# Attention and gated MLP in one kernel: the second product of a head pair issued in two runs, its V load and its x^T store placed later

## The chip, the cores and the metric

The kernel runs on one NeuronCore of a Trainium2 chip. The metric is the device time of one execution in microseconds (us). Engines are named as in the profile: PE (matrix engine, with PEld for its weight loads), DVE (vector), ACT (scalar), POOL (GpSimd) and SP (which here only issues DMAs).

## The reference

Causal attention in blocks of 64, then a gated MLP without biases, all in float32:

```
scores = q @ k^T / sqrt(64), masked where block(query) < block(key)      # 8 batches, 8 heads, 576 x 64
attn   = exp(scores - max) / (sum + 1e-9)
x      = (attn @ v), heads side by side                                    # 4608 x 512
out    = (sigmoid(x @ w_gate) * (x @ w_val)) @ w_out                        # 512 -> 1536 -> 512
```

## The kernel before

Matrix operands are split into a high and a low part and a product is summed from three matmuls (high by high, high by low, low by high), so that 128x512 matmuls run in a fast form and keep precision. The names end in H and L for the two parts.

**Stages.** The heads are taken in 32 pairs (two heads of one batch). The loop over pairs near the end of the kernel runs one period for each pair. While attention runs, matmuls of the MLP's first four column chunks are dealt in between (L153 for gate and value, L160 for the output product), at a rate worked out from what is left over the places ("ticks") of a period. After the last pair the rest of that MLP part follows, and then the remaining eight chunks in ten passes (L1110, L1195).

**Order of a period.** The tables at the top (lines 28 to 36) write out the order by hand: a name and the number of ticks of MLP work dealt after it. Pairs 0 to 6 go by `FIRST` and `ALONE`, pair 7 by `TURN`, pair 8 by `JOIN`, pairs 9 to 31 by `REST`. The steps of a `REST` period are these.

- `AV`: the product of the previous pair's probabilities with V (`z_av`, L583). `s`: this pair's scores (`s_blocks`), on PE, with a mask, a row maximum (L434) and exponentials on ACT (L442) behind them. `t`: the scores of the last 64 queries, the tail (L307 with operands QBH and QBL), which need the bank of the first scores again and so wait for its exponentials.
- `tr3`, `tr2`, `trl`, `trt`: DVE transposes of the probabilities of query blocks 3, 2, 1 with 0, and the tail into the tile Z (L568, L576, L579). Z and one of the two V buffers lie in one tile, ZV; the other V buffer is VR1. Even pairs use VR1, odd pairs the one in ZV.
- `k` and `q`: the next pair's K and Q are transposed on DVE and split on ACT and DVE (L341, L378 to L383), and the loads of K and Q for the pair three further on are issued.
- `r`: the reciprocals of the sums (L494 to L499), written to DRAM (r_d, L502) and read back spread over the partitions (rb, L507 and L508).
- `FX`: `finish` of the previous pair: POOL multiplies x^T by rb (L629), ACT splits off the high part (L631), the store of x^T to DRAM is issued on ACT's queue (L636), and POOL makes the low part (L638).

**Queues.** A scheduler orders the instructions of each engine. `behind(a, b)` forbids it to place a ahead of b on the same engine, and `line(engine, a)` chains the instructions of an engine in program order. On PE the scores, the dealt MLP matmuls and the AV product are chained in that way. The V load (L246, two heads into 32 partitions, then L248 copies them to the other 96) has no such tie, nor has the store of x^T.

**AV.** Each pair takes 18 key blocks of 32 keys, four row groups and two heads, so 144 matmuls, each recorded as two matmul and two weight-load instructions, into four PSUM banks:

```
order = [*range(4), 16, 17, *range(4, 16)]
for n, kb in enumerate(order):
    ...
            matmul(pv[a // 2][rows(h), a % 2, lo:144], lhsT=VR[at_rows, h, kb],
```

**Later weights.** In the first five passes, `do_later` (L1263) converts 24 pieces of the weights of the second five, and stores them to DRAM (wgv_d, wo_d). Its count is by place of the pass and by unit in it. After the fifth pass the output weights are loaded from wo_d into the one tile wo (L1328), which the sixth pass needs.

Of the kernel before, what the change touches and what calls it, by code (L numbers as in the profile page):

```python
# [20 lines left out]
N2 = 512  # L21
# [10 lines left out]
JOIN = (("s", 3), ("t", 1), ("AV", 2), ("tr3", 1), ("tr2", 1), ("k", 0), ("trl", 1), ("trt", 1), ("r", 0), ("q", 3))  # L32
REST = (("AV", 0), ("s", 3), ("t", 3), ("tr3", 1), ("tr2", 1), ("k", 0), ("FX", 0), ("trl", 1), ("trt", 1), ("r", 0), ("q", 2))
# [9 lines left out]
def attn_glu_kernel(ctx: ExitStack, tc: tile.TileContext, q, k, v, w_gate, w_val, w_out, out):  # L43
# [142 lines left out]
    with ExitStack() as s2:  # L186
# [53 lines left out]
        def load(p, what, queue=nc.sync):  # L240
            b, hp = pairs[p]
            h0 = 2 * hp
            if what == "v" and p > N_FIRST:
                VR = VRs[(p + 1) % 2]
                for h in range(2):
                    nc.sync.dma_start(out=VR[0:32, h], in_=v[b, h0 + h].rearrange("(t p) d -> p t d", p=32))  # L246
                for a in range(1, 4):
                    dma = nc.sync.dma_start(out=VR[32 * a:32 * a + 32], in_=VR[0:32])  # L248
                loads["SP"] = dma.ins
                return  # L250
# [151 lines left out]
        def attend(p):  # L402
# [88 lines left out]
            def recip():  # L491
# [12 lines left out]
                if rest:  # L504
                    tails = r_f[4 * P:5 * P].rearrange("(a h r) -> a h r", a=4, h=2)
                    for h in range(2):
                        nc.sync.dma_start(out=rb[rows(h), 0:4 * P], in_=r_f[5 * P * h:5 * P * h + 4 * P].partition_broadcast(D))  # L507
                        nc.sync.dma_start(out=rb[rows(h), 4 * P:S].rearrange("p (a r) -> p a r", a=4),  # L508
                                          in_=tails[:, h].partition_broadcast(D))
                    return  # L510
                for h, o, n, f in ((0, 0, S, 0), (1, 4 * P, D, S), (1, 0, 4 * P, S + D)):
                    dma = nc.sync.dma_start(out=rb[rows(h), o:o + n], in_=r_f[f:f + n].partition_broadcast(D))
                rb_last[:] = [dma.ins] if p < N_FIRST else []
# [69 lines left out]
            def z_av():  # L583
                pv = [two_banks(), two_banks()]
                VR = VRs[(p + 1) % 2]
                order = [*range(4), 16, 17, *range(4, 16)]
                for n, kb in enumerate(order):
                    g = kb // 4
                    lo, z = (32 * g, ZB * (kb % 4) + (ZG + 32) * g) if g < 4 else (P, 2 * P + 16 * (kb % 4))
                    for a in range(4):  # L590
                        at_rows = slice(32 * a, 32 * a + 32)
                        for h in range(2):
                            matmul(pv[a // 2][rows(h), a % 2, lo:144], lhsT=VR[at_rows, h, kb],
                                   rhs=Z[at_rows, ZH * h + z:ZH * h + z + 144 - lo],
                                   start=(n == 0), stop=(n == len(order) - 1), tile_position=(32 * a, 64 * h))
                            if n == a == h == 0:
                                for ins in recent:
                                    behind(pe_last[0], ins)
                hold[:] = pe_last
                for t, (engine, copy) in enumerate((("ACT", nc.scalar.copy), ("DVE", nc.vector.tensor_copy))):  # L600
# [23 lines left out]
            def finish():  # L624
# [9 lines left out]
                if p == len(pairs) - 1:  # L634
                    mark("ACT", cut)
                (nc.sync if NP <= p <= N_FIRST else nc.scalar).dma_start(  # L636
                    out=xT_d[b, hp * P:(hp + 1) * P, :], in_=xT)
                nc.gpsimd.tensor_sub(out=XL[:, hp, :w], in0=xT[:, :w], in1=XH[:, hp, :w].bitcast(F32))  # L638
# [11 lines left out]
            def step(what):  # L650
# [18 lines left out]
                elif rest and what == "trt":  # L669
                    z_tail()  # L670
                elif what == "tr3":
# [10 lines left out]
                elif what == "av":  # L682
                    if rest:
                        z_av()
                        return
# [577 lines left out]
        def do_later(k, i):  # L1263

            place = turns_of[0].index(k)
            count = 2 * (0 if place == 0 or blocks[k][1] < N2 else i < 4 if place == 1 else i in (0, 1, 3) if place == NK - 1
                         else 1)
# [90 lines left out]
```

## Time and profile before

| | us |
|---|---|
| median of 3 runs | 1306.68 |
| lowest and highest run | 1300.39, 1309.89 |
| profiled execution, time | 1306.74 |
| profiled execution, span of the core's instructions | 1305.0 |
| PE busy in it | 1156.9 (89%) |
| periods of pairs 9 to 31 with the end of pair 8's, about | 145.5 to 655.3 |

The time of the profiled execution stands 1.7 us above its span, and at the median of the runs. An engine's busy time is a sum over stages with different limits, so what a change is worth is read from the stage in which it lies. "Idle before" in a row is the time in which an engine stood still ahead of those instructions, with what ended it; "issue" means that nothing the profile shows was waited for.

### The profile page before, as it was taken

The page shows a single profiled execution, that of the slowest core. Times are in us where ns is not written, and L with a number is a line of the kernel's source. Part 1 is how long each engine was busy: PE and PEld are TensorE (multiplying, and loading weights), DVE is VectorE, ACT ScalarE, POOL GpSimd, SP SyncE. Part 2 cuts the span into 40 slices and gives each one's busy share as a digit, 9 for nine tenths or more (in the row PEclk, how much of TensorE's full clock was granted, in tenths as well). Part 3 has the DMA queues.
Part 4 walks back from the last instruction along what each step waited for, and adds up shares of the span by engine and source line. Part 5 has one row for each costly group of instructions (what it writes and reads, how often), then busy time and mean ns, then how long its engine had stood idle before and what let it go on. Part 6 is the DMA issues. An engine that isn't in the chain of part 4 may idle for free.

```text
span 1305.0 us, 30506 instructions
## 1 busy us (share of the span) xinstructions
PE 1156.9 (89%) x12073; PEld 934.8 (72%) x12073; DVE 928.4 (71%) x1844; ACT 547.0 (42%) x1274; POOL 334.9 (26%) x380
## 2 busy tenths in 40 slices
PE   8799788877688878787798999999999969999998
PEld 5466576666566656665676888888888758888888
DVE  5778666665575757565788695887988876767665
ACT  5677444343343434252424444354454422333222
POOL 3355332222231322222330120111120133342502
PEclk9899999998899989889999999999999989999999
DMA  7666555655555546463523314264277747262532
GB/s 167 170 147 154 122 127 128 135 121 123 112 112 140 115 109 144 95 141 92 152 84 109 117 49 130 49 192 131 69 208 264 250 161 234 67 208 89 178 98 80
DMA packets 314687, 175.31 MB, mean 134 GB/s; under 512 B 239152, under 2 KB 279088, under 8 KB 311600
## 3 DMA queue, kind: packets, MB, share of 16 engines
q1 hardware_dynamic: 303744, 154.84, 47.0%
q10 hardware_dynamic: 10416, 17.47, 3.8%
q8 instruction: 95, 1.56, 0.5%
q0 software_dynamic: 384, 1.05, 0.2%
q14 instruction: 48, 0.39, 0.1%
HBM read 104.73 MB, written 47.33 MB: 117 GB/s over the span
## 4 chain that ended last, share of the span: by engine, by line
PE 55%; DVE 16%; DMA 11%; issue 8%; SPq 4%; ACT 4%; POOL 2%; ACTq 0%; DVEq 0%; POOLq 0%
PE b L1110 21%; PE bank L307 10%; PE m L153 6%; PE b L1195 6%; PE m L1195 6%; DVE ZV L568 3%; DMA rb<-r_d 3%; PE m L160 2%; DMA r_d<-rT 2%; ACT P L442 2%; DMA part_d<-ost 1%; SPq L278 1%; POOL xT L629 1%; SPq L502 1%; DVE KQ L341 1%
## 5 line engine op out<-in xcount | busy, mean ns | idle before, releaser
L1110 PE MATMUL b<-XH,w 128*128 128x512 f32 (+1 forms) x1120 | 321.9, 369 | 1.9 <-DVE p L1156 0.5
L1110 PEld LDWEIGHTS b<-XH,w 128*128 128x128 f32 x1120 | 203.5, 188 | 40.3 <-DVE p L1156 1.4
L1110 PE MATMUL b<-XL,w 128*128 128x512 f32 (+1 forms) x560 | 205.8, 368 | 0.0
L442 ACT ACTIVATE P<-bank,nm 128x512 f32<-128x512 f32 (+3 forms) x256 | 131.8, 538 | 122.0 <-POOL xT L629 74.7
L1110 PEld LDWEIGHTS b<-XL,w 128*128 128x128 f32 x560 | 105.6, 189 | 17.4
L942 ACT CAST XH<-XB 128x1024 fp32r<-128x1024 f32 (+1 forms) x72 | 67.2, 945 | 94.6 <-DVE XB L940 49.4
L434 DVE TENSOR_REDUCE nm<-bank 128x2 f32<-128x1024 f32 (+3 forms) x128 | 102.5, 822 | 3.1
L1195 PE MATMUL m<-wo,hH 128*128 128x512 f32 x288 | 95.0, 396 | 10.2 <-DMA wo<-wo_d 10.2
L307 PE MATMUL bank<-ZV 32*64 32x144 f32 (+5 forms) x3680 | 76.5, 264 | 28.2 <-issue 28.2
L160 PE MATMUL m<-wo,hH 128*128 128x512 f32 x256 | 90.2, 419 | 12.3 <-DVE h L172 9.7
L307 PEld LDWEIGHTS bank<-ZV 32*64 32x64 f32 (+1 forms) x3680 | 62.7, 136 | 45.7 <-issue 34.2
L1195 PE MATMUL b<-wo,hH 128*128 128x512 f32 x288 | 93.0, 389 | 0.0
L153 PE MATMUL m<-XH,wv 128*128 128x512 f32 x240 | 85.5, 415 | 4.9 <-ACT t L170 4.1
L945 DVE TENSOR_TENSOR XL<-XB,XH 128x1024 fp32r<-128x1024 f32 (+1 forms) x72 | 80.1, 1115 | 13.7 <-ACT XH L942 12.0
L927 POOL TENSOR_TENSOR XB<-XB 128x256 f32<-128x256 f32 x30 | 23.7, 790 | 251.1 <-DMA XB<-xT_d 126.1
L601 DVE COPY xT<-bank 128x256 f32<-128x256 f32 x24 | 10.2, 425 | 107.7 <-PE bank L307 107.7
L153 PE MATMUL m<-XH,wg 128*128 128x512 f32 x240 | 83.3, 404 | 1.8 <-ACT ost L778 1.8
L568 DVE STREAM_TRANSPOSE ZV<-P 128x512 f32<-128x512 f32 (+1 forms) x192 | 80.1, 476 | 0.0
L629 POOL TENSOR_TENSOR xT<-xT,rb 128x576 f32<-128x576 f32 x24 | 34.0, 1417 | 169.5 <-DMA rb<-r_d 80.8
L1195 PEld LDWEIGHTS m<-wo,hH 128*128 128x128 f32 x288 | 55.2, 192 | 22.2 <-DMA wo<-wo_d 10.6
L160 PEld LDWEIGHTS m<-wo,hH 128*128 128x128 f32 x256 | 51.6, 203 | 27.1 <-DVE h L172 11.8
L485 DVE TENSOR_REDUCE nm<-bank 128x1 f32<-128x576 f32 x32 | 24.2, 756 | 65.3 <-PE bank L307 65.3
(214 smaller groups left out, 2535.4 us busy)
## 6 DMA issues: line engine op xcount, KB each, us to landing
XB<-xT_d SPq DMA_DIRECT2D x48, 256.0 KB
prr<-part_d SPq DMA_DIRECT2D x46, 256.0 KB
VR<-VR SPq DMA_DIRECT2D x36, 288.0 KB
ZV<-ZV SPq DMA_DIRECT2D x36, 288.0 KB
part_d<-ost SPq DMA_DIRECT2D x36, 256.0 KB
part_d<-ost ACTq DMA_DIRECT2D x32, 256.0 KB
xT_d<-xT ACTq DMA_DIRECT2D x28, 288.0 KB
rqk<-in_k_dram SPq DMA_DIRECT2D x108, 72.0 KB
```

What stands on the lines that cost most here:

```text
L153: mm = nc.tensor.matmul(ps, lhsT=lh, rhs=rh, start=(i == 0), stop=(i == n - 1))
L160: mm = nc.tensor.matmul(ps, lhsT=lh[:, f, t * P:(t + 1) * P], rhs=rh, start=(f == i == 0), stop=(f == F1 - 1 and i == 2))
L307: pe_last[:] = [nc.tensor.matmul(*args, **kw).ins]
L434: line("DVE", nc.vector.tensor_reduce(out=nm[:, c0:c0 + 2], in_=ps[:, :, c:c + P * (i + 1)], axis=AX.X, op=ALU.max, negate=True), rest)
L442: line("ACT", nc.scalar.activation(out=Pi[:, h], in_=ps[:, h, c:c + n], func=AF.Exp, bias=nm[:, c0 + h:c0 + h + 1], accum_out=sm[:, 5 * h ...
L485: line("DVE", nc.vector.tensor_reduce(out=nm[:, c0:c0 + 1], in_=ps[:, :, :288], axis=AX.XY, op=ALU.max, negate=True), rest)
L568: line("DVE", nc.vector.transpose(out=dst[:, :, :4 * ZG].rearrange("p b (g x) -> p b g x", g=4)[:, :, :i + 1, :32], in_=Pi[:, h].rearrange ...
L629: nc.gpsimd.tensor_mul(out=xT, in0=xT, in1=rb)
L942: cut = nc.scalar.copy(out=XO[j][0][:, a:b, c], in_=x)
L945: sub = nc.vector.tensor_sub(out=XO[j][1][:, a:b, c], in0=x, in1=XO[j][0][:, a:b, c].bitcast(F32))
L1110: mm = nc.tensor.matmul(ps, lhsT=lh, rhs=rh, start=(first and k == 0), stop=(k == n - 1), skip_group_check=not first)
L1195: mm = nc.tensor.matmul(po[t], lhsT=lh[:, f, t * P:(t + 1) * P], rhs=rh, start=(half == 0 and i == 0), stop=(half == 1 and i == 5))
```

## The change

AV of a pair is issued in two runs. A new step `half` in the pair's own period takes key blocks 8 to 17 (80 matmuls), as soon as `tr3`, `tr2` and `trt` are done; the following period's `AV` takes blocks 0 to 7 (64 matmuls) into the same banks and then copies x^T out. In the tables `trt` moves ahead of `half`, `trl` and `k` behind it, and the ticks are shared out anew. The first DMA of a V load is put behind the last rb load of the period before, and the store of x^T is chained on ACT in program order, behind the split of the high part. In the later passes, two of the 24 weight conversions move from the fifth pass to the end of the second.

```
-JOIN = (("s", 3), ("t", 1), ("AV", 2), ("tr3", 1), ("tr2", 1), ("k", 0), ("trl", 1), ("trt", 1), ("r", 0), ("q", 3))
-REST = (("AV", 0), ("s", 3), ("t", 3), ("tr3", 1), ("tr2", 1), ("k", 0), ("FX", 0), ("trl", 1), ("trt", 1), ("r", 0), ("q", 2))
+JOIN = (("s", 3), ("t", 1), ("AV", 2), ("tr3", 1), ("tr2", 1), ("trt", 1), ("half", 0), ("trl", 1), ("k", 0), ("r", 1), ("q", 1))
+REST = (("AV", 0), ("s", 3), ("t", 2), ("tr3", 1), ("tr2", 1), ("trt", 2), ("half", 0), ("trl", 1), ("k", 0), ("FX", 0), ("r", 1), ("q", 1))
...
-                    nc.sync.dma_start(out=VR[0:32, h], in_=v[b, h0 + h].rearrange("(t p) d -> p t d", p=32))
+                    behind(nc.sync.dma_start(out=VR[0:32, h], in_=v[b, h0 + h].rearrange("(t p) d -> p t d", p=32)).ins,
+                           loads["rb"])
...
+                    loads["rb"] = dma.ins
...
-            def z_av():
-                pv = [two_banks(), two_banks()]
+            pv = []
+
+            def z_half(second):
+                if not pv:
+                    pv.extend(two_banks() for _ in range(2))
                 VR = VRs[(p + 1) % 2]
-                order = [*range(4), 16, 17, *range(4, 16)]
-                for n, kb in enumerate(order):
+                for n, kb in enumerate((0, 4, 1, 5, 2, 6, 3, 7) if second else (8, 12, 9, 13, 10, 14, 11, 15, 16, 17)):
                     g = kb // 4
                     lo, z = (32 * g, ZB * (kb % 4) + (ZG + 32) * g) if g < 4 else (P, 2 * P + 16 * (kb % 4))
                     for a in range(4):
                         at_rows = slice(32 * a, 32 * a + 32)
                         for h in range(2):
+                            first = n == 0 and not second
                             matmul(pv[a // 2][rows(h), a % 2, lo:144], lhsT=VR[at_rows, h, kb],
-                                   rhs=Z[at_rows, ZH * h + z:ZH * h + z + 144 - lo],
-                                   start=(n == 0), stop=(n == len(order) - 1), tile_position=(32 * a, 64 * h))
+                                   rhs=Z[at_rows, ZH * h + z:ZH * h + z + 144 - lo], start=first,
+                                   stop=(n == (7 if second else 9)), tile_position=(32 * a, 64 * h), skip_group_check=second)
                             if n == a == h == 0:
                                 for ins in recent:
                                     behind(pe_last[0], ins)
                 hold[:] = pe_last
+
+            def z_out():
...
-                (nc.sync if NP <= p <= N_FIRST else nc.scalar).dma_start(
+                store = (nc.sync if NP <= p <= N_FIRST else nc.scalar).dma_start(
                     out=xT_d[b, hp * P:(hp + 1) * P, :], in_=xT)
+                if rest:
+                    line("ACT", store)
...
+                elif what == "half":
+                    z_half(False)
...
-                        z_av()
+                        z_half(True)
+                        z_out()
...
-            count = 2 * (0 if place == 0 or blocks[k][1] < N2 else i < 4 if place == 1 else i in (0, 1, 3) if place == NK - 1
-                         else 1)
+            count = 0 if place == 0 or blocks[k][1] < N2 or place == NK - 1 and i > 1 else 2
```

Lines of the changed kernel stand from 1 to 12 further down than those of the kernel before. On PE, before, around the end of pair 24's period: the last dealt MLP matmuls, pair 24's whole AV product (operands ZV for Z, VR for V) and the first scores of pair 25 (KH, QH).

```order
L160 MATMUL m<-wo,hH 128x512
L153 MATMUL m<-XH_1011,wg_117 128x512
L153 MATMUL m<-XL_1012,wg_117 128x512
L153 MATMUL m<-XH_1011,wg_117 128x512 x2
L307 MATMUL bank<-ZV,VR_95 64x144 x32
L307 MATMUL bank<-ZV,VR_95 64x16 x16
L307 MATMUL bank<-ZV,VR_95 64x112 x32
L307 MATMUL bank<-ZV,VR_95 64x80 x32
L307 MATMUL bank<-ZV,VR_95 64x48 x32
L307 MATMUL bank<-KH,QH 128x512 x2
```

The same place now, from the end of the first run to the opening of the second.

```order
L308 MATMUL bank<-ZV,VR_95 64x48 x8
L308 MATMUL bank<-ZV,VR_95 64x16 x16
L160 MATMUL m<-wo,hL 128x512
L160 MATMUL m<-wo,hH 128x512 x2
L160 MATMUL m<-wo,hL 128x512
L160 MATMUL m<-wo,hH 128x512
L153 MATMUL m<-XH_1011,wg_117 128x512
L153 MATMUL m<-XL_1012,wg_117 128x512
L153 MATMUL m<-XH_1011,wg_117 128x512 x2
L308 MATMUL bank<-ZV,VR_95 64x144 x8
L308 MATMUL bank<-ZV,VR_95 64x112 x8
```

The one run of 144 matmuls has become runs of 80 and 64 with nine MLP matmuls between them.

On SP, before, from pair 18's reciprocals (r_d) on: the V load that follows them fills VR, the buffer of even pairs, so it is pair 20's.

```order
L502 DMA r_d<-rT 9x32 x4
L507 DMA rb<-r_d 64x512
L508 DMA rb<-r_d 64x4x16
L507 DMA rb<-r_d 64x512
L508 DMA rb<-r_d 64x4x16
L246 DMA VR_95<-in_v_dram 32x18x64 x2
L248 DMA VR_95<-VR_95 32x2304 x3
L278 DMA rqk_92<-in_k_dram 32x18x32 x4
L278 DMA rqk_92<-in_q_dram 32x18x32 x4
L502 DMA r_d<-rT 9x32 x4
```

SP now, from the same pair 18's reciprocals on.

```order
L503 DMA r_d<-rT 9x32 x4
L279 DMA rqk_93<-in_q_dram 32x18x32 x2
L508 DMA rb<-r_d 64x512
L509 DMA rb<-r_d 64x4x16
L508 DMA rb<-r_d 64x512
L509 DMA rb<-r_d 64x4x16
L279 DMA rqk_93<-in_q_dram 32x18x32 x2
L246 DMA ZV<-in_v_dram 32x18x64 x2
L249 DMA ZV<-ZV 32x2304 x3
L279 DMA rqk_92<-in_k_dram 32x18x32 x4
L503 DMA r_d<-rT 9x32 x4
```

The V load there now fills the buffer in ZV, that of the next, odd pair 19: it comes one period later than before, and two pairs of Q loads have moved around the rb loads.

On ACT, before, at a period's opening: the copies of x^T out of PSUM, the store, then the exponentials.

```order
L631 CAST XH_1011<-xT 128x512
L177 CAST hH<-h_5970 128x512
L601 COPY xT<-bank 128x2x4x32
L603 COPY xT<-bank 128x32
L636 DMA xT_d<-xT 128x576
L442 ACTIVATE P_6162,sm_108<-bank,nm 128x512 x2
```

ACT now, at the same pair's opening.

```order
L639 CAST XH_1011<-xT 128x512
L644 DMA xT_d<-xT 128x576
L177 CAST hH<-h_6042 128x512
L609 COPY xT<-bank 128x2x4x32
L611 COPY xT<-bank 128x32
L443 ACTIVATE P_6162,sm_108<-bank,nm 128x512 x2
```

Before, the store stands between the copies and the exponentials; now a pair's store stands right behind the split of its high part (CAST), at the end of the period.

## Rows read from the trace of the kernel before

**Rows 1.** Busy time of each engine by stretch: the AV periods, a later stop.

```profile
core 0: us, PE busy (x) PEld busy (x) DVE busy (x) ACT busy (x) POOL busy (x), PEclk, DMA share, GB/s
...
145.50:655.30 509.80, 403.44 (x8081) 330.11 (x8065) 321.33 (x718) 201.77 (x598) 130.37 (x182) 0.92 0.55 123
...
1054.60:1064.90 10.30, 0.08 (x2) 0.07 (x1) 10.30 (x13) 3.29 (x5) 4.63 (x3) 0.74 0.92 332
```

**Rows 2.** PE groups from 145.5 to 655.3 us: busy, mean ns, idle before.

```profile
L307 PE MATMUL bank<-ZV,VR 32*64 32x144 f32 (+4 forms) x3412 | 49.3, 250 | 23.2 <-issue 23.2
L307 PE MATMUL bank<-ZV 32*64 32x144 f32 (+4 forms) x3168 | 48.0, 258 | 26.1 <-issue 26.1
...
L307 PE MATMUL bank<-KH,QBH 128*128 128x288 f32 x46 | 16.5, 359 | 34.6 <-issue 19.8 <-ACT P L442 14.9
```

**Rows 3.** PE in order of time, pair 18's AV to pair 19's tail: start, length.

```profile
367.97 2.75 PE L307 MATMUL bank<-ZV,VR 32*64 32x144 f32 x182
372.40 1.56 PE L307 MATMUL bank<-ZV,VR 32*64 32x80 f32 x106 [1.68 <-issue]
373.89 0.79 PE L307 MATMUL bank<-KH,QH 64*128 64x512 f32 x2
...
380.57 0.37 PE L307 MATMUL bank<-KH,QBH 128*128 128x288 f32 x1 [0.99 <-issue]
...
381.44 0.39 PE L153 MATMUL m<-XL,wv 128*128 128x512 f32 x1
...
382.12 0.39 PE L153 MATMUL m<-XL,wv 128*128 128x512 f32 x1
```

**Rows 4.** Busy time of PE, and the DMA queue of its instructions (packets, MB, share).

```profile
PE 1156.9 (89%) x12073; PEld 934.8 (72%) x12073; DVE 928.4 (71%) x1844; ACT 547.0 (42%) x1274; POOL 334.9 (26%) x380
...
q8 instruction: 95, 1.56, 0.5%
```

**Rows 5.** The stretch of pair 19's scores, columns as in rows 1.

```profile
373.90:377.30 3.40, 3.40 (x25) 2.99 (x23) 2.09 (x6) 0.41 (x2) 0.16 (x1) 0.56 0.46 112
```

**Rows 6.** ACT in order of time, the x^T store and pair 19's first exponentials.

```profile
378.60 0.33 ACTq L636 DMA_DIRECT2D xT_d<-xT  x1
379.02 0.69 ACT L442 ACTIVATE P<-bank,nm 128x512 f32<-128x512 f32 x1 [4.71 <-POOL xT L629]
```

**Rows 7.** Waits, 145.5 to 655.3 us: total, times, longest.

```profile
ACT P L442 <- POOL xT L629: 74.7, 13, 8.1
```

**Rows 8.** DVE in order of time in pair 19's period.

```profile
381.64 0.76 DVE L485 TENSOR_REDUCE nm<-bank 128x1 f32<-128x576 f32 x1 [2.02 <-PE bank L307]
382.32 2.21 DVE L568 STREAM_TRANSPOSE ZV<-P 128x512 f32<-128x512 f32 x4
...
386.81 0.85 DVE L576 STREAM_TRANSPOSE ZV<-Pt 128x128 f32<-128x128 f32 x4
...
388.73 0.21 DVE L499 STREAM_TRANSPOSE rT<-sm 128x32 f32<-128x32 f32 x1
```

**Rows 9.** SP's DMA issues in order of time, from pair 18's reciprocals on.

```profile
368.61 1.04 SPq L278 DMA_DIRECT2D rqk<-in_q_dram  x2
369.76 1.42 SPq L502 DMA_DIRECT2D r_d<-rT  x4
...
374.64 1.81 SPq L246 DMA_DIRECT2D VR<-in_v_dram  x2
379.09 2.11 SPq L248 DMA_DIRECT2D VR<-VR  x3
```

**Rows 10.** Stretches in which these V copies end, columns as in rows 1.

```profile
383.10:384.10 1.00, 1.00 (x6) 0.84 (x5) 1.00 (x3) 1.00 (x4) 0.00 (x0) 1.00 1.27 265
384.10:385.10 1.00, 1.00 (x6) 0.79 (x6) 1.00 (x2) 0.32 (x2) 0.00 (x0) 1.00 0.13 28
```

**Rows 11.** The stop on wo: the PE group, and SP's store and load.

```profile
L1195 PE MATMUL m<-wo,hH 128*128 128x512 f32 x288 | 95.0, 396 | 10.2 <-DMA wo<-wo_d 10.2
...
1051.84 0.43 SPq L1002 DMA_DIRECT2D wo_d<-st  x1
...
1057.06 0.32 SPq L1328 DMA_DIRECT2D wo<-wo_d  x1
```

More of the change, by code (lines that the diff above doesn't have):

```diff
@@ L507, in recip @@
                         nc.sync.dma_start(out=rb[rows(h), 0:4 * P], in_=r_f[5 * P * h:5 * P * h + 4 * P].partition_broadcast(D))
-                        nc.sync.dma_start(out=rb[rows(h), 4 * P:S].rearrange("p (a r) -> p a r", a=4),
-                                          in_=tails[:, h].partition_broadcast(D))
+                        dma = nc.sync.dma_start(out=rb[rows(h), 4 * P:S].rearrange("p (a r) -> p a r", a=4),
+                                                in_=tails[:, h].partition_broadcast(D))
+                    loads["rb"] = dma.ins
                     return
@@ L512, in recip @@
                     dma = nc.sync.dma_start(out=rb[rows(h), o:o + n], in_=r_f[f:f + n].partition_broadcast(D))
+                loads["rb"] = dma.ins
                 rb_last[:] = [dma.ins] if p < N_FIRST else []
```

## The prediction

> **What bounds the kernel now.** I read the busy time by stretch first. From 145.5 to 655.3 us, 23 periods of 22.2 us, PE is busy 403.4 of 509.8 us and idle 106.4; DVE is busy 63% [rows 1]. So PE with its stops is the limit there, at 17.5 us of work and 4.6 us of idling a period. Then I read PE's groups for what it idles at. Ahead of AV's own matmuls it stands 23.2 + 26.1 = 49.3 us, all "issue"; ahead of the tail scores 34.6 us; some 22.5 us are left for all else [rows 1, 2]. The timeline shows one of each: pair 18's AV runs 2.75 us, stops for 1.68 us in its middle, runs on for 1.56; pair 19's tail waits 0.99 us [rows 3].
>
> *The stop in AV.* Nothing is waited for, so it is PE's own supply. PE's 24,146 instructions come in 95 packets on queue 8, so 254 to a packet [rows 4]. AV's 288 matmul records take 2.75 + 1.56 us, 15.0 ns each, and each has its weight load, so a packet of 254 instructions lasts 1.9 us in AV. An MLP matmul takes (382.12 - 381.44) / 3 = 0.227 us [rows 3], and there a packet lasts 29 us. I read the stop as the next packet coming too late when a whole one has gone by at AV's pace.
>
> *The wait of the tail.* It needs the first scores' exponentials. On ACT these stand behind the store of x^T, which waits for POOL's product with rb: the store goes out at 378.60, the exponentials 0.4 us later, after 4.71 us of idling [rows 6]. ACT idles 74.7 us in 13 such waits [rows 7].
>
> [...]
>
> **The change part by part**, against the profiled execution, 1306.7 us, which stands at the median.
>
> *AV in two runs: 39 us saved.* A run of 576 instructions has on average (576 - 254) / 254 = 1.27 packet ends that follow a packet used up at AV's pace. 49.3 us over 23 pairs is 2.1 us a pair, so 1.7 us for each such end. The first run now has 80 matmuls, 320 instructions: (320 - 254) / 254 = 0.26. The second has 64, 256 instructions: none. Between them stand nine MLP matmuls, 2.0 us, in which a packet can come. So 49.3 falls by a factor of 0.26 / 1.27, to 10, and 39 are saved. Bounds: 49.3 saved if no stop is left, nothing if each run has its own.
>
> *The store behind the split: 30 us saved.* Exponentials no longer wait for POOL. Of 34.6 us I leave 4.6 for tails that come before ACT is done anyway. Bounds: 0 and 34.6. Behind the store on ACT now stand the MLP's activations and the next copies of x^T; the split ahead of it needs the same product of POOL, a period after the copies, so it waits for nothing new.
>
> *What PE must wait for at the first run.* It needs the transposes of blocks 3, 2 and the tail. After the tail's maximum ends (381.64 + 0.76 = 382.4) these take 2.21 + 0.85 us and a short fifth one, some 3.3 us in all, to 385.7 [rows 8]; K and Q's transposes now come later. PE has 2 + 1 + 1 + 2 ticks of about three MLP matmuls behind the tail, 18 x 0.227 = 4.1 us from 381.6: also 385.7. I cost it at nothing, but no slack covers it. DVE's order keeps its length, so the low parts of K and Q, at its end, are ready as before.
>
> *V one period later: 12 us lost.* Before, V was there a period early. Now its load follows the rb loads of the period before its use, and two Q loads, and the first run waits for its copies. From the issue of r_d to the V load 374.64 - 369.76 = 4.9 us; two Q loads more, 1.0; to the copies 4.45; and the copies' bytes move until about 384.9, 5.8 us after issue [rows 9, 10]. In all 16.2 us from reciprocal to V. On PE wait the MLP matmuls and the next period behind it. The loop goes over two periods: 16.2, then the first run (160 records x 15.0 ns = 2.4, and 0.5 of stop), nine MLP matmuls 2.0, the second run 1.9, and from the next scores' start to their reciprocals 388.94 - 373.89 = 15.05, less the tail's 0.99, 14.1 [rows 3, 8]. That is 37.1 us, so a period is not under 18.5. Without V, the savings above and 8 of the clock leave (509.8 - 39 - 30 - 8) / 23 = 18.8. The two are so near that, as each varies, V will be late in part of the periods: I take 0.5 us a period, 12. Bounds: 0; and, with the two hops as long as the store and load of wo (5.2 and 7.8 us [rows 3, 11] in place of 4.45 and 5.8; the load ends where its 10.2 us of waiting end, 1064.8 [rows 1]), the loop is 39.9, a period 19.9, 26 us lost.
>
> *The clock: 8 us saved.* [...] Fewer stops should mean fewer falls, but waits for V are stops too. Bounds: 10 lost, 41 saved; I stay near the lower, as one stop of 1.68 us was enough here [rows 3, 5].
>
> *Two conversions earlier: 5 us saved.* PE stands 10.2 us for wo. Its last piece is stored from 1051.84, the load goes out at 1057.06, and PE has been ready since 1054.6 [rows 1, 11]. With two pieces less ahead, the store can go earlier. Bounds 0 and 10.2, I take half. At the second pass DVE has that work more, beside PE's products; I cost it at nothing, and at up to those 10.2 us if products wait for DVE.
>
> *Sum:* 1306.7 - 39 - 30 + 12 - 8 - 5 = 1236.7, so 1237 us; a period goes from 22.2 to 19.3. By the terms' bounds I hold 1208 to 1265 for this case.
>
> **The rivals.**
>
> *V never late, the clock nearly whole.* With the 41 us regained, 403.4 - 41 + 22.5 + 10 + 4.6 = 399.5 us, 17.4 a period; less wo, 1306.7 - 110 - 5 = 1192. Against it speaks the loop of 18.5. 8%.
>
> *The stops in AV are not the packets.* Then cutting the run leaves 49.3 us in place, the period stays at (509.8 - 30) / 23 = 20.9, V is in time, and 1306.7 - 30 - 5 = 1272. For it: "issue" names no cause. Against: a stop of much the same length in the middle of nearly every AV. 12%. [...]
>
> *V takes the place of what is removed.* If K, Q and rb traffic stretch reciprocal to V by 6 us, the loop is 43, a period 21.5, and 1306.7 - 15 - 5 = 1287; by 7 us, 1298, within 1%. 9% for the latter.
>
> *Slower.* The same loop gives a period over 22.2 us once reciprocal to V passes 44.4 - 20.9 = 23.5 us. At 26 us it is 23.45: 1306.7 + 29 - 5 = 1331. What could do it is the one SP queue: V load, its wait, copies and K loads now stand in one row ahead of the next reciprocals. Against: in the rows the same hops take 16.2. 7%.
>
> *The change does nothing.* The first run could stand so late in PE's order that both form one run; the order shows nine MLP matmuls between, so I give it no share of its own.
>
> **How the numbers follow.** The forecast has 64%, so with the first two rivals faster by over 1% (below 1293.6; about what a measurement of this kernel can tell) has 0.64 + 0.08 + 0.12 = 0.84; within 1% 0.09; slower 0.07. For 8 in 10 I leave out the slower cases (0.16) and the lowest few: 1200 to 1287.
>
> **What would show it.** Right: AV's idle before falls to about 10 us, and the tail's below 8; no wait of ACT for POOL's x^T; a new wait of PE's first run for V's copies, under 1 us a period; about 19.3 us between reciprocals; PE's stop for wo about 5. Wrong: stops in both runs of AV; PE waiting 2 us and more for V in most periods, or for DVE's tail transposes; a granted clock under 0.92; new stops of PE in the second or third pass of the later chunks.

## The result and the profile after

| | before | changed |
|---|---|---|
| median, us (4 runs each, on the same chip) | 1305.16 | 1266.46 |
| lowest and highest, us | 1300.39, 1309.89 | 1263.20, 1269.53 |
| ratio, 95% interval | | 0.970 (0.966 to 0.975) |
| profiled execution: time, span, us | 1306.74, 1305.0 | 1269.53, 1267.7 |

The change is faster by 38.7 us, where 70 were forecast; 1266 lies in the range of 1200 to 1287, 29 us above the 1237, and just outside the 1208 to 1265 that the prediction held by its terms' bounds.

First the stretches. To have the same stretches in every kernel they run here from the first tail scores of pair 8 to the end of the last AV (the AV stage), and from the first matmul of the ten passes to the last matmul. The two rows of before:

```profile
133.44:662.57 529.13, 419.80 (x8474) 342.35 (x8474) 335.30 (x753) 210.41 (x622) 136.82 (x189) 0.92 0.55 123
...
743.13:1301.15 558.02, 546.16 (x2544) 455.88 (x2544) 429.49 (x784) 215.03 (x359) 127.79 (x114) 0.99 0.48 146
```

The same of the changed kernel (columns as in [rows 1]):

```profile
128.98:644.49 515.51, 436.34 (x8483) 352.22 (x8483) 311.04 (x753) 212.93 (x622) 146.33 (x189) 0.88 0.58 127
...
720.54:1263.55 543.01, 542.49 (x2544) 454.67 (x2544) 424.61 (x784) 214.48 (x359) 125.09 (x114) 1.00 0.49 150
```

The AV stage, where 65 of the 70 us were to come from, gave 13.6. PE idles 79.2 us in it instead of 109.3, but is busy 16.5 us longer, at a granted clock of 0.88 instead of 0.92. The ten passes gave 15.0. The rest of the 37.6 us up to the last matmul is 4.5 in what lies between the two stretches and 4.5 in the first 130 us; the latter is no more than this beginning differs among the kernels run below (127.2 to 137.1 us).

PE's groups in that stage of the changed kernel, which answer to [rows 2] (busy, mean ns, idle before; L308 is L307 of before):

```profile
L308 PE MATMUL bank<-ZV,VR 32*64 32x80 f32 (+4 forms) x3456 | 63.5, 275 | 36.6 <-DMA VR<-VR 27.2 <-issue 6.3 <-ACT wo L142 2.8
...
L308 PE MATMUL bank<-ZV 32*64 32x48 f32 (+5 forms) x3484 | 62.7, 267 | 24.7 <-DMA ZV<-ZV 14.6 <-issue 6.9 <-DVE ZV L579 2.5
...
L308 PE MATMUL bank<-KH,QH 64*128 64x512 f32 (+1 forms) x138 | 27.8, 393 | 11.2 <-ACT xT L611 10.3 <-issue 0.6 <-PE bank L308 0.3
...
L308 PE MATMUL bank<-KH,QBH 128*128 128x288 f32 x48 | 14.4, 301 | 0.7 <-POOL wo L143 0.7
```

The stops without a cause ("issue") ahead of AV fell to 6.3 + 6.9 = 13.2 us; in before they are 28.2 + 23.2 = 51.4 over this stretch. The tail's wait is gone: 0.7 us, from 35.3. The groups of before:

```profile
L307 PE MATMUL bank<-ZV 32*64 32x80 f32 (+5 forms) x3484 | 55.4, 259 | 28.2 <-issue 28.2
L307 PE MATMUL bank<-ZV,VR 32*64 32x144 f32 (+4 forms) x3456 | 50.0, 250 | 23.2 <-issue 23.2
...
L307 PE MATMUL bank<-KH,QBH 128*128 128x288 f32 x48 | 17.2, 358 | 35.3 <-issue 19.8 <-ACT P L442 14.9 <-POOL wo L143 0.7
```

But PE now waits 27.2 + 14.6 = 41.8 us for V's copies, and 10.3 us at a period's second scores for ACT's copies of x^T, a wait that [rows 2] did not have. PE in order of time, from pair 24's first run:

```profile
479.86 0.77 PE L308 MATMUL bank<-ZV,VR 32*64 32x80 f32 x12
482.31 1.81 PE L308 MATMUL bank<-ZV,VR 32*64 32x80 f32 x148 [1.68 <-DMA VR<-VR]
...
486.31 2.38 PE L308 MATMUL bank<-ZV,VR 32*64 32x144 f32 x128
488.62 0.50 PE L308 MATMUL bank<-KH,QH 64*128 64x512 f32 x2
...
492.16 0.69 PE L308 MATMUL bank<-KH,QH 64*128 64x384 f32 x2 [2.58 <-ACT xT L611]
```

The first run starts, meets the row group whose copy has not landed, and stands. SP's issues from the next reciprocals on, which answer to [rows 9]:

```profile
484.01 2.08 SPq L503 DMA_DIRECT2D r_d<-rT  x4
486.13 0.88 SPq L279 DMA_DIRECT2D rqk<-in_q_dram  x2
487.99 0.48 SPq L508 DMA_DIRECT2D rb<-r_d  x1
...
491.63 1.33 SPq L279 DMA_DIRECT2D rqk<-in_q_dram  x2
493.06 1.29 SPq L246 DMA_DIRECT2D ZV<-in_v_dram  x2
497.26 1.99 SPq L249 DMA_DIRECT2D ZV<-ZV  x3
```

From r_d to the V load it takes 9.05 us here; over 23 periods the mean is 7.67, where 4.9 + 1.0 was forecast. The 4.88 us that [rows 9] show for this hop is the shortest one in the trace of before: over pairs 8 to 29 its mean there is 6.61 us and the longest is 9.69. ACT in the same place, which answers to [rows 6]:

```profile
482.61 0.33 ACTq L644 DMA_DIRECT2D xT_d<-xT  x1
...
485.51 0.60 ACT L791 ACTIVATE ost<-m 128x512 f32<-128x512 f32 x1 [1.86 <-PE m L160]
491.21 0.34 ACTq L794 DMA_DIRECT2D part_d<-ost  x1
491.65 0.37 ACT L609 COPY xT<-bank 128x256 f32<-128x256 f32 x1 [5.54 <-DMA rb<-r_d]
```

The store of x^T goes out without a wait. But the next DMA on ACT, the store of the MLP's partial sums (part_d), has its data at 486.11 and goes out at 491.21, and the copies of x^T, whose banks the second scores need, stand behind it. What they copy is complete at 488.69, when the second run ends. The program's order, with what each instruction waits for, shows why (ACT, one such place):

```
L644 DMA xT_d<-xT 128x576
L791 ACTIVATE ost<-m 128x512 [waits DMAHW7_49,PE_49]
L794 DMA part_d<-ost 128x512 [waits DMAHW4_49,Activation_49]
L609 COPY xT<-bank 128x2x4x32 [waits DMAHW2_49,PE_49]
L611 COPY xT<-bank 128x32
```

In the trace of the change the 984 DMAs that SP issues and the 67 that ACT issues count on the same eight semaphores. This store's wait is for one of them, DMAHW4 in the order above: it ended at 491.14, when the rb load that SP had issued at 487.99 on the same semaphore had landed, and the store went out at 491.21. So this store of ACT's waited for an rb load of SP's, with which it has nothing else to do.

The stop on wo is gone; its group, which answers to [rows 11] (L1208 is L1195 of before):

```profile
L1208 PE MATMUL m<-wo,hH 128*128 128x512 f32 x288 | 93.2, 389 | 0.0
```

PE idles 0.5 us in all ten passes together, so the second and third show no new stop.

### The profile page after: what moved, and what is told of

It is laid out like the page before. It is cut to its first block, busy times and chain, and to the rows that moved or that the text cites. A ratio compares the mean times of both kernels' runs of the same rounds, so it can differ in the third digit from the quotient of the medians.

```text
span 1267.7 us, 30599 instructions
## 1 busy us (share of the span) xinstructions
PE 1166.6 (92%) x12073; PEld 941.5 (74%) x12073; DVE 899.1 (71%) x1844; ACT 548.3 (43%) x1274; POOL 341.6 (27%) x380
## 4 chain that ended last, share of the span: by engine, by line
PE 68%; DMA 11%; DVE 8%; SPq 5%; issue 3%; ACT 3%; POOL 1%; ACTq 0%; DVEq 0%
PE b L1123 26%; PE bank L308 11%; PE m L1208 8%; PE b L1208 8%; PE m L153 8%; PE m L160 4%; DMA VR<-VR 3%; PE bank L153 2%; DMA ZV<-ZV 2%; ACT P L443 2%; SPq L279 2%; DMA r_d<-rT 1%; DMA rb<-r_d 1%; DVE ZV L571 1%; DMA ZV<-in_v_dram 1%
## 5 line engine op out<-in xcount | busy, mean ns | idle before, releaser
L1123 PEld LDWEIGHTS b<-XH,w 128*128 128x128 f32 x1120 | 203.5, 188 | 37.6 <-ACT p L1141 0.8
L308 PE MATMUL bank<-ZV 32*64 32x48 f32 (+5 forms) x3680 | 83.8, 272 | 24.7 <-DMA ZV<-ZV 14.6
L308 PEld LDWEIGHTS bank<-ZV 32*64 32x64 f32 (+1 forms) x3680 | 66.9, 142 | 47.7 <-DMA ZV<-ZV 16.9
L609 DVE COPY xT<-bank 128x256 f32<-128x256 f32 x24 | 10.2, 425 | 127.1 <-PE bank L308 127.1
L308 PE MATMUL bank<-ZV,VR 32*64 32x80 f32 (+4 forms) x3456 | 63.5, 275 | 36.6 <-DMA VR<-VR 27.2
L1208 PE MATMUL m<-wo,hH 128*128 128x512 f32 x288 | 93.2, 389 | 0.0
L308 PEld LDWEIGHTS bank<-ZV,VR 32*64 32x64 f32 x3456 | 55.8, 151 | 50.0 <-DMA VR<-VR 25.1
L1208 PE MATMUL b<-wo,hH 128*128 128x512 f32 x288 | 92.9, 389 | 0.0
L958 DVE TENSOR_TENSOR XL<-XB,XH 128x1024 fp32r<-128x1024 f32 (+1 forms) x72 | 78.4, 1092 | 13.5 <-ACT XH L955 13.3
L153 PE MATMUL m<-XH,wg 128*128 128x512 f32 x240 | 87.3, 421 | 0.4 <-ACT t L170 0.4
L160 PEld LDWEIGHTS m<-wo,hH 128*128 128x128 f32 x256 | 53.2, 209 | 15.1 <-ACT hH L177 2.9
```

What stands on the lines that cost most here:

```text
L153: mm = nc.tensor.matmul(ps, lhsT=lh, rhs=rh, start=(i == 0), stop=(i == n - 1))
L160: mm = nc.tensor.matmul(ps, lhsT=lh[:, f, t * P:(t + 1) * P], rhs=rh, start=(f == i == 0), stop=(f == F1 - 1 and i == 2))
L308: pe_last[:] = [nc.tensor.matmul(*args, **kw).ins]
L958: sub = nc.vector.tensor_sub(out=XO[j][1][:, a:b, c], in0=x, in1=XO[j][0][:, a:b, c].bitcast(F32))
L1123: mm = nc.tensor.matmul(ps, lhsT=lh, rhs=rh, start=(first and k == 0), stop=(k == n - 1), skip_group_check=not first)
L1208: mm = nc.tensor.matmul(po[t], lhsT=lh[:, f, t * P:(t + 1) * P], rhs=rh, start=(half == 0 and i == 0), stop=(half == 1 and i == 5))
```

## The experiments

Each ran beside the kernel before on one chip, but not all on the same chip: the medians of before are 1305.2 to 1310.0 us there, so that kernels of different chips are better compared by their ratios. "Stops" are the idle times of PE ahead of AV with "issue" as their cause, in the AV stage.

| kernel | median, us | ratio to before (95%) |
|---|---|---|
| the change | 1266.5 | 0.970 (0.966 to 0.975) |
| e4, store alone | 1278.9 | 0.977 (0.973 to 0.981) |
| e5, conversions alone | 1293.3 | 0.989 (0.984 to 0.994) |
| e8, store and conversions, AV whole | 1259.9 | 0.963 (0.960 to 0.965) |
| e6, AV split in place alone | 1290.8 | 0.987 (0.982 to 0.991) |
| e10, e6 with store and conversions | 1249.8 | 0.954 (0.952 to 0.957) |
| e1, the change, V early | 1240.6 | 0.947 (0.943 to 0.951) |
| e9, the change, V ahead of Q | 1268.0 | 0.968 (0.964 to 0.972) |
| e7, e1 with K and Q loads late | 1262.7 | 0.965 (0.962 to 0.967) |
| e11, e1, part_d on POOL | 1225.3 | 0.936 (0.930 to 0.941) |
| e12, e7, part_d on POOL | 1242.8 | 0.951 (0.946 to 0.955) |
| e13, e9, part_d on POOL | 1241.1 | 0.949 (0.945 to 0.953) |
| e14, e11 without V copies (work left out) | 1195.1 | 0.912 (0.907 to 0.917) |

### e1: the V load not held back

```diff
-                    behind(nc.sync.dma_start(out=VR[0:32, h], in_=v[b, h0 + h].rearrange(...)).ins,
-                           loads["rb"])
+                    nc.sync.dma_start(out=VR[0:32, h], in_=v[b, h0 + h].rearrange(...))
```

> The changed kernel, with its V load no longer held behind the rb loads; in SP's order this moves nothing but which pair the load is for: it becomes that of the pair after next, one period earlier, as in the kernel before. Theory (the chain reciprocal, r_d, rb, V load, V copies, first run sets the period in the changed kernel): PE's 41.8 us of waiting for V's copies fall below 5, the stretch from the first AV pairs to the last AV (515.5 us in the changed kernel, 529.2 before) falls to about 450 to 470, and the time to 1205 to 1225. Rival (V is only the last of several things that come late together): the waits for V turn into waits for scores, transposes or the low parts of K and Q, the stretch stays over 500 us, and the time within 15 us of the changed kernel's 1266. Rival (SP: the load now waits on SP for the buffer that the second run frees, and K loads and reciprocals queue behind it): K loads and r_d go out later, the time is over 1275.

Measured: 1240.6 us, between the theory's time and the rival's. The AV stage and two of its groups:

```profile
135.49:614.59 479.10, 416.26 (x8483) 337.02 (x8483) 310.74 (x753) 213.05 (x622) 146.59 (x189) 0.94 0.63 134
```

```profile
L307 PE MATMUL bank<-ZV 32*64 32x48 f32 (+5 forms) x3484 | 58.9, 261 | 13.2 <-issue 12.7 <-DVE ZV L578 0.3
L307 PE MATMUL bank<-ZV,VR 32*64 32x80 f32 (+4 forms) x3456 | 56.3, 261 | 24.8 <-issue 21.7 <-DVE ZV L578 2.8
```

V's waits are gone, all 41.8 us. PE's busy time fell by 20.1 us with them, the clock going from 0.88 to 0.94: those waits had cost clock too. The stage is 36 us shorter. It missed 450 to 470 because the stops rose from 13.2 to 12.7 + 21.7 = 34.4 us. Twelve instruction packets stop PE in e1 and not in the change. In the change only two of them moved during a wait for V, so those waits hid few of them. What differs is the traffic beside them: from 2 us before each packet until it has landed, other transfers keep the DMA engines busy 0.95 of the time in e1 and 0.53 in the change. e14 below tests this.

### e4, e5, e8: the other two parts, alone and together

e4, and e8 with e5's edit added:

```diff
-                (nc.sync if NP <= p <= N_FIRST else nc.scalar).dma_start(
+                store = (nc.sync if NP <= p <= N_FIRST else nc.scalar).dma_start(
                     out=xT_d[b, hp * P:(hp + 1) * P, :], in_=xT)
+                if rest:
+                    line("ACT", store)
```

> The kernel before, with only the store of x^T chained on ACT behind the split. Theory (the store ahead of the exponentials made the tail late): PE's idle before the tail scores falls from 34.6 us to under 5, the AV stops stay at 45 to 55 us, the time falls by 15 to 30 us to 1275 to 1290. Rival (the tail's wait is hidden slack that comes back at the next wait): the tail's idle goes, but the time stays within 8 us of 1305.

e5:

```diff
-            count = 2 * (0 if place == 0 or blocks[k][1] < N2 else i < 4 if place == 1 else i in (0, 1, 3) if place == NK - 1
-                         else 1)
+            count = 0 if place == 0 or blocks[k][1] < N2 or place == NK - 1 and i > 1 else 2
```

> The kernel before, with only the two weight conversions moved. Theory: PE's stop for wo falls from 10.2 us to under 2, and the time by about 10 us to 1295. Rival (the stop was there in one execution, or the conversions cost at the end of the second pass what they give): within 5 us of 1305.

> The kernel before with the store of x^T chained and the conversions moved, but AV whole and V early: the change without its first part. If the parts add up, 1309 - 30 - 13 gives 1262 to 1270, so that the split with its later V (1266 in the changed kernel) is worth nothing by itself. Rival (the split is worth its 39 us in the changed kernel, and the store and the conversions don't add up): 1280 or more here.

The store alone: 1278.9, 30.1 us under before. Its tail group and one AV group:

```profile
L307 PE MATMUL bank<-ZV 32*64 32x80 f32 (+5 forms) x3484 | 60.4, 275 | 30.8 <-issue 30.8
...
L307 PE MATMUL bank<-KH,QBH 128*128 128x288 f32 x48 | 14.2, 296 | 0.7 <-POOL wo L143 0.7
```

The tail's 34.6 us are gone, as in the theory. The stops grew from 51.4 to 60.0 us (29.2 in the other group). The conversions alone: 1293.3, 15.7 us under before, with an interval of about 8 to 21. Their row of the ten passes, and the group of wo:

```profile
742.72:1287.47 544.75, 543.12 (x2544) 454.62 (x2544) 425.89 (x784) 213.24 (x359) 127.52 (x114) 1.00 0.49 150
```

```profile
L1195 PE MATMUL m<-wo,hH 128*128 128x512 f32 x288 | 93.2, 389 | 0.0
```

The 10.2 us of waiting are gone, and 3.0 us of PE's busy time, which in before ran at a lower clock (0.99 against 1.00). The two together: 1259.9, 49.7 us under before, where the sum is 45.8. So they add up within these intervals, and the change without its first part is not slower than the whole change: 0.963 against 0.970. The split with its later V load gave nothing, or took up to 1%.

### e6, e10: AV split in place

AV stays whole at the opening of the next period, with V early, and gets MLP matmuls into its middle.

```diff
-REST = (("AV", 0), ("s", 3), ..., ("r", 0), ("q", 2))
+REST = (("AVh", 2), ("AV", 0), ("s", 3), ..., ("r", 0), ("q", 0))
...
-                for n, kb in enumerate(order):
+                for n, kb in list(enumerate(order))[10:] if second else list(enumerate(order))[:10]:
```

> The kernel before, with AV still whole at the opening of the next period, but two of its ticks of MLP matmuls (about six to eight) moved from ahead of it into its middle, after 80 of the 144 matmuls; V, store and conversions as before. Theory (a whole packet of 254 instructions used up at AV's pace makes the stop): idle before AV's matmuls falls from 49.3 us to 8 to 16, the time by 25 to 40 us to 1265 to 1280. Rival (the stop has another cause, in AV's operands or banks): the idle stays at 40 to 50 us, the time within 10 us of 1305.

> The kernel before with the store chained, the conversions moved, and AV split in place (80 matmuls, two ticks of MLP matmuls, 64 matmuls, all at the opening of the next period, V early): the change without moving a run into the pair's own period. If the packets are the stop and the tail no longer waits, AV's idle is 8 to 15 us, the tail's under 5, and the time 1222 to 1240, under the changed kernel's 1266. Rival (the stop removed from AV comes back as another wait of PE, as at the tail in e6_split_in_place, where the time fell by only 18 us): 1250 or more.

e6:

```profile
L307 PE MATMUL bank<-ZV 32*64 32x144 f32 (+5 forms) x3484 | 61.8, 275 | 4.8 <-issue 4.0 <-DVE ZV L576 0.5
L307 PE MATMUL bank<-ZV,VR 32*64 32x144 f32 (+4 forms) x3456 | 52.5, 249 | 9.0 <-issue 4.5 <-DVE ZV L576 4.4
...
L307 PE MATMUL bank<-KH,QBH 128*128 128x288 f32 x48 | 19.8, 413 | 56.4 <-issue 33.2 <-ACT P L442 22.5 <-POOL wo L143 0.7
```

The stops fell from 51.4 to 8.5 us with nothing but six to eight MLP matmuls put into the run: it was how densely AV's instructions follow each other. But the time fell by only 18 us to 1290.8, out of the theory's 1265 to 1280: 21 us came back at the tail, which still waited for the store of x^T and was now reached sooner. With the store out of the way (e10) the time is 1249.8, 10 us under e8, but over the theory's 1240. The stops there are 11.5 + 17.8 = 29.3 us, where 8 to 15 were expected, though the order within AV is that of e6; this opened the question of e7 and e14.

### e9, e13: V ahead of the Q loads

```diff
+                    if what == "r" and N_FIRST <= p and p + 1 < n:
+                        load(p + 1, "v")
...
+                    if what == "q" and "V" in loads:
+                        behind(dma.ins, loads["V"])
```

> The changed kernel, with the V load still behind the rb loads of the period before its use, but ahead of all four Q loads, two of which stood between r_d and rb, and two between rb and V. Theory (the V load comes late because two Q loads stand ahead of it, and because its DMA issue waits for an earlier Q load to land): from the first r_d to the V load 7.7 us falls to 4.5 to 5.5, the waits for V's copies fall from 41.8 us to 15 to 25, the time to 1245 to 1258. Rival (the hop is the round trip through r_d and rb, whatever stands between): the hop stays over 7 us, the time within 6 us of 1266.

> e9_v_before_q with the same stores on POOL's queue. Theory (V ahead of the Q loads was worth its 20 us of V waits, and the time stayed only since ACT's stores took 30.6 us in its place): the time falls to 1235 to 1250, V's waits stay at 15 to 28. Rival (without ACT's wait V's are the limit again, since the loop over two periods sets the pace): V's waits rise to 30 or more, the time stays over 1255.

In e9 the hop from r_d to V fell from 7.67 to 5.93 us, a little above the theory's 5.5, and V's waits from 41.8 to 20.2 + 1.2 = 21.4 us. The time did not move:

```profile
L312 PE MATMUL bank<-ZV,VR 32*64 32x80 f32 (+4 forms) x3456 | 62.3, 274 | 31.8 <-DMA VR<-VR 20.2 <-issue 6.0 <-ACT wo L142 2.8
...
L312 PE MATMUL bank<-KH,QH 64*128 64x512 f32 (+1 forms) x138 | 28.2, 405 | 30.9 <-ACT xT L615 30.6 <-PE bank L312 0.3
```

The 20 us came back as 20 more of waiting for ACT's copies of x^T, behind part_d's store. The theory was near on the hop, right on V's waits and wrong on the time. The 1.7 us that the hop lost are less than the 0.88 + 1.33 us for which SP issues the two pairs of Q loads in the rows above; that the issue also waited for a Q load to land, as the theory said, the runs do not show. In e13, with that store on POOL, the time falls by 27 us to 1241.1, and V's waits are 31.3 + 8.6 = 39.9 us: the theory's time, with the rival's waits. V's copies are again what PE waits for longest; that the loop through V sets the period there fits this and was not tested further.

### e7, e12: K and Q loads behind rb

```diff
-                    if p >= N_FIRST and p + 3 < n:
-                        load(p + 3, what)
+                    if p >= N_FIRST and p + 3 < n and what == "q":
+                        load(p + 3, "k")
+                        load(p + 3, "q")
...
+                    if p > N_FIRST + 3:
+                        behind(dma.ins, loads["rb"])
```

> The kernel e1_v_free (the changed kernel with V a period early), with all eight K and Q loads of a period put behind its rb loads instead of around the reciprocals. In e1_v_free PE still stops 34.4 us for nothing the profile names in AV, against 8.5 us in e6_split_in_place, and its instruction packets then arrive beside K loads and V copies. Theory (the packet comes late because it shares the DMA engines with those transfers): the stops fall to 10 to 20 us and the time to 1215 to 1230. Rival (the stops are set by the distance of the packet ends in PE's own order alone): 30 to 40 us stay, the time within 8 us of 1240.

> e7_k_late with the same stores on POOL's queue. Theory (in e7_k_late the packet stops of AV fell from 34.4 to 21 us, and the gain was eaten by 34.8 us of waiting for x^T's copies, behind those stores on ACT): the waits fall below 5, the stops stay at 18 to 25, the time falls by 25 to 40 us to 1222 to 1238. Rival (the banks are late by themselves, since K and Q loads crowd the opening): over 20 us of waiting for x^T stay, the time over 1250.

In e7 the stops fell from 34.4 to 7.5 + 13.6 = 21.1 us, near the theory's 20, but 34.8 us of waiting for x^T's copies came, and the time rose to 1262.7, which neither side expected:

```profile
L310 PE MATMUL bank<-KH,QH 64*128 64x512 f32 (+1 forms) x138 | 29.9, 429 | 35.2 <-ACT xT L613 34.8 <-issue 0.4
```

In e12 those fall to 8.5 us, the stops to 7.9 + 8.6 = 16.5, and the time to 1242.8, above the theory's 1238: PE now waits 11.8 us for DVE's transposes and 22.2 us for the MLP's split on ACT, against 2.8 and 3.4 in e7. On the same chip e12 is 17.5 us slower than e11 below, so the loads are no better placed there.

### e11: the stores of part_d on POOL's queue

```diff
-                    nc.scalar.dma_start(out=part_d[r:r + P, :], in_=ost)
+                    nc.gpsimd.dma_start(out=part_d[r:r + P, :], in_=ost)
```

> e1_v_free, with the stores of the MLP's partial sums (part_d, of the attention stage) issued on POOL's queue instead of ACT's. Theory (these stores stop ACT until a DMA of SP's queue has landed, and with it the copies of x^T that free the banks of the scores): PE's 10.0 us of waiting for x^T's copies go, the time falls by 8 to 15 us to 1225 to 1233. Rival (POOL pays for the issues and delays the low parts or x^T): the time stays within 6 us of 1240 or rises.

```profile
133.28:600.19 466.91, 412.87 (x8483) 333.11 (x8483) 311.53 (x753) 212.14 (x622) 160.63 (x214) 0.94 0.64 138
```

```profile
L307 PE MATMUL bank<-ZV 32*64 32x48 f32 (+5 forms) x3484 | 58.8, 260 | 13.3 <-issue 11.5 <-DVE ZV L578 1.7
L307 PE MATMUL bank<-ZV,VR 32*64 32x80 f32 (+4 forms) x3456 | 54.4, 252 | 21.8 <-issue 19.0 <-DVE ZV L578 2.8
...
L307 PE MATMUL bank<-KH,QH 64*128 64x512 f32 (+1 forms) x138 | 26.5, 377 | 0.5 <-issue 0.5
```

The 10.0 us that e1 waited there are 0.5, and the time falls by 15.2 us to 1225.3: the fastest kernel of the study that does the whole work, 6.4% under before and some 3.5% under the change. POOL is busy 14.0 us longer than in e1, and PE's wait for its low parts of the MLP's h (hL) stays as it was: 9.7 us, against 9.8.

### e14: no copies of V

```diff
-                for a in range(1, 4):
+                for a in range(1, 4) if p < 12 else ():
```

> e11_v_free_pool without the three copies of V to the other row groups from pair 12 on, so AV there multiplies by the rows left from earlier pairs: work is left out, 864 KB of transfers a pair; PE's order in the attention stage stays word for word. In e11_v_free_pool AV still stops 30.5 us with no releaser, while six-tenths of that with the same number of matmuls in a run was seen in no kernel of quieter DMA queues (8.5 us in e6_split_in_place). Theory (the instruction packet comes late because the V copies, which then fill the DMA engines, run beside it): the stops fall to 8 to 18 us, the time by 10 to 20 us to 1205 to 1216. Rival (the distance of packet ends in PE's order sets the stops, whatever moves beside): 26 to 34 us stay; a small gain of under 6 us may come from elsewhere.

e11's pair whose second run begins at 205.57, and the DMA share around it:

```profile
205.57 1.52 PE L307 MATMUL bank<-ZV 32*64 32x144 f32 x83
208.86 0.91 PE L307 MATMUL bank<-ZV 32*64 32x112 f32 x45 [1.77 <-issue]
```

```profile
200.30:208.90 8.60, 6.43 (x262) 5.30 (x261) 3.75 (x9) 2.48 (x5) 4.35 (x8) 1.00 0.89 175
```

The same pair in e14:

```profile
205.45 2.17 PE L307 MATMUL bank<-ZV 32*64 32x144 f32 x128
```

```profile
200.77:207.60 6.83, 6.83 (x302) 5.92 (x301) 3.71 (x9) 2.48 (x6) 4.00 (x8) 1.00 0.49 105
```

The DMA engines are busy 0.49 instead of 0.89 and the stop is not there. Over the stage:

```profile
L307 PE MATMUL bank<-ZV 32*64 32x48 f32 (+5 forms) x3484 | 58.9, 265 | 6.7 <-issue 6.5
L307 PE MATMUL bank<-ZV,VR 32*64 32x80 f32 (+4 forms) x3456 | 52.3, 254 | 6.5 <-issue 3.7 <-DVE ZV L578 2.8
```

10.2 us of stops against 11.5 + 19.0 = 30.5 in e11, with PE's instructions in the same order. The packet behind the stop shown moves from 206.62 to 207.56 us in e11; in e14 it moves from 203.46 to 204.80, ahead of the run. Thirteen packets stop PE in e11 and not in e14: with V's copies, other transfers keep the DMA engines busy 0.93 of the time from 2 us before such a packet until it has landed, without them 0.46, and on average the packet starts to move 97 of PE's instructions ahead of its first one instead of 166. So what PE lacks at a stop comes by DMA, and it comes later when V's copies run beside it. The time fell more than expected, by 30 us to 1195.1. The stage is 30.6 us shorter: 20.3 are stops, 8.8 are PE's busy time (404.07 us), 1.4 is all other idling.

## Why the prediction was right in its sign and off in its size

**AV in two runs: 39 us saved, to 10 of stops.** The stops were 13.2 us, and 10.2 where V's copies don't run beside AV. The cause holds, and the traces show it directly. Count the instructions that a trace records of PE, its semaphore waits among them: each of the 29 stops of before comes when 449 plus a multiple of 256 of them have started, and each ends 1.2 to 1.8 us after a packet of 16 KB on queue 8 has landed. The same is true of all 246 stops in the fourteen kernels. For the stop of [rows 3], from 370.72 to 372.40, the packet moves from 369.99 to 370.95; the queue's line for 369.9 to 371.0 us:

```profile
q8 instruction: 1, 0.02, 5.4%
```

So the rival that they are not the packets is out. In none of the fourteen kernels does a packet start to move more than 297 instructions ahead of its first one.

What the step lacked is that the fetch's time depends on the other transfers: in e1 and e11 the same two runs stop for 34.4 and 30.5 us. That the change came so near to 10 is in part luck, for with its late V load the DMA engines were quieter ahead of the packets (0.53 against 0.95 busy with other transfers, as under e1).

**The store: 30 us saved.** Alone it gave 30.1 us (e4), and the tail's wait is gone in the change. Right. The wait for DVE's transposes at the first run, put at nothing, was small too: PE waited 2.5 us for them, once.

**Two conversions earlier: 5 saved.** The term of half the stop was too small: all of the 10.2 us went, and 3.0 us of PE's busy time with it; alone 15.7 us (e5), of which 13.3 lie in the ten passes. The bound of 10.2 left out the clock.

**V one period later: 12 us lost.** This is the step that failed, and in its size. "In all 16.2 us from reciprocal to V": measured are 1.73 us from the reciprocal to r_d's issue, which the step put at nothing, 7.67 from r_d to the V load (5.9), 4.47 to the copies (4.45), and 6.67 from the copies' issue to the end of PE's last wait for them (5.8), so 20.5. With its other terms as they were, the loop "37.1 us, so a period is not under 18.5" becomes 41.4 and 20.7. The reciprocals of pairs 9 and 30 in the changed kernel:

```profile
165.08 0.21 DVE L500 STREAM_TRANSPOSE rT<-sm 128x32 f32<-128x32 f32 x1
...
608.28 0.21 DVE L500 STREAM_TRANSPOSE rT<-sm 128x32 f32<-128x32 f32 x1
```

443.2 / 21 = 21.1 us a period, where 19.3 was forecast. With the last pair, 31, it is 21.5, against 22.1 in before over the same pairs. In e1, without the hold, pairs 9 and 30 give 19.9, so it is the loop through V that sets the period.

Half of the missing 4.3 us could have been read in the trace of before. The prediction took each hop from pair 18 alone, and its 4.88 us is the shortest of its kind there. By the means over pairs 8 to 29 the hops are 0.59, 6.61 and 4.27; with the prediction's 1.0 and 5.8 that is 18.3. The other half, 2.2 us, came with the change, but not in the hop from r_d to V: 6.61 + 1.0 would have been right there. 1.1 of it lies ahead of r_d's issue and 0.9 behind the issue of V's copies; what stretched these two is open.

The rival "V takes the place of what is removed" had the right mechanism for this stage: a period of 21.5 for 6 us more. It is partly luck that the time is inside the range all the same: with the stage's 13.6 us and the 5 forecast for the passes, the profiled 1306.7 would have become 1288, over 1287. Ten more in the passes and the 4.5 + 4.5 outside both stretches, which no term named, brought it in. Taking the hold away (e1) gives 26 us.

**The clock: 8 us saved.** PE was busy 16.5 us longer in the stage, outside the bound of 10 lost. No run shows the 8 us, or the 41 that are its other bound and that the first rival takes whole. What the trace of before shows is 83.9 us of the 509.8 of [rows 1] at a granted clock of 0.50, where 128x512 matmuls follow each other every 0.427 us, against 0.227 at 1.00. Over the whole stage 85.3 us are at 0.50 there, and 126.3 in the changed kernel. The term that "stops for V are stops too" was there, but the sum had 12 us for V's lateness, and V's waits were 41.8. In e1 without them the clock is 0.94.

**A wait not foreseen.** "Behind the store on ACT now stand the MLP's activations and the next copies of x^T" looked at one store of ACT's and not at the other. The 10.3 us for x^T's copies are part_d's store; e11 shows it for the like 10.0 us of e1 by moving that store. The trace of before had the wait already (its waits, and its group of the first scores, over the same stretch):

```profile
ACT xT L601 <- DMA rb<-r_d: 11.6, 2, 6.6
```

```profile
L307 PE MATMUL bank<-KH,QH 64*128 64x512 f32 (+1 forms) x138 | 30.8, 436 | 1.0 <-PE bank L307 1.0
```

ACT stood there 11.6 us in two places, and PE lost nothing by it, so that it was passed over.

Together, in the profiled executions: 38.2 us of stops and 34.6 of the tail's waiting gone, 41.8 for V and 10.3 for x^T come, 9.4 fewer of all other idling, 16.5 more of PE's busy time, 13.6 in all; 15.0 in the passes, and the 4.5 + 4.5 above.

## What to carry to other kernels

A load that is moved nearer to its use must be priced with the hops of the period in which it will run, from the first thing it is behind to the last byte, with each issue that stands ahead of it on its queue; here 16.2 us were 20.5, and the loop over two periods took back 26 of the 68 us that the rest of the change gives (e1). Such a hop is read as a mean over many periods, not from one: the one chosen here was the shortest of 22. A DMA issued on a compute engine can stop that engine for reasons that lie on another queue, as the rb load of SP's stopped ACT for 5.54 us in the change; here the stores did better on POOL (15 to 27 us in e11, e12 and e13). And parts of a change should be run alone: here two of three carried the gain, and one line of the third cost 26 us.

## What the runs showed of the hardware beyond that

- PE's instructions come in packets of 256 (24,310 recorded instructions and 95 packets in before), and a stop without a named cause inside a run of short matmuls was a packet that had not come: 246 of 246 stops lie at packet ends, and PE goes on 1.2 to 1.8 us after the packet has landed.
- The supply of PE's instructions shares the DMA engines (from 369.9 to 371.0 us in before one packet took 5.4% of them and other transfers 75.1%): the same order stopped 30.5 us with V's copies beside it and 10.2 without (e11, e14).
- In the change a DMA of ACT's waited until one of SP's on the same semaphore had landed: ACT stood 5.54 us there, the last 3.0 of them ahead of copies whose data were complete. PE waited 34.8 us for such copies in e7, and 8.5 in e12 with the stores on POOL; in e1 and e11 it was 10.0 and nothing.
- Waits cost twice: with V's 41.8 us of waiting PE's own work took 20.1 us longer, at a granted clock of 0.88 instead of 0.94 (the change and e1).
